# The data's Fourier transform reads the loaded data as two 64-column operands instead of one of 128 from a rearranged copy

## The chip, the cores and the metric

The kernel runs on one core of a Trainium2 chip. The metric is the device time of one execution in microseconds. The five engines are called as in the profile: PE (matrix products; PEld is its loading of the stationary operand), DVE and ACT (the two engines that also read PSUM, where PE writes), POOL, and SP, which here issues nearly all transfers.

## The reference, cut to what matters

The output is a gated mix `g * a + (1 - g) * b` of two branches on the same input x (2048 positions, 512 channels).

```python
g = sigmoid((x * gate_w).sum(-1, keepdims=True))
# branch a: a long convolution along the positions
P = exp(logdA[:, :, None] * l[None, None, :])
K = einsum("dn,dnl,dn->dl", Cc, P, dB).real            # filters, 512 x 2048, from 128 complex states
y = irfft(rfft(u padded to 4096) * rfft(K padded to 4096))[:, :, :L]
a = y + u * Dskip
# branch b: linear attention, 32 heads of 16
q, k, v = x @ wqkv;  pq = q @ w_phi;  pk = k @ w_phi
phi(z) = concat(softmax(z), softmax(-z))
o = (phi(q) @ (phi(k)^T v)) / (phi(q) @ sum phi(k) + 1e-6)
b = o @ wo
```

Both branches are computed in bf16 with f32 sums in PSUM.

## The kernel before

**How the work is listed and ordered.** The class `Plan` holds a list of nodes. Each node names its engine (or two, of which one is chosen), its dependences and the buffers that it takes and drops. `Plan.run` emits the nodes in the order that the long string ORDER gives, two characters a node. The string SIDES chooses, for each node that may run on either of two engines, which one (0 the first, 1 the second). RINGS chooses between two PSUM pools, WARM adds spare matmuls (none here), and FOURS says for each of 16 filter units whether its products are summed by DVE or by PE. So the order on each engine, SP's queue too, is a table written out in advance; each engine works through its own list, and waits where an operand is not there.

**The tables (0 to some 30 us).** `prepare` makes the Fourier tables: W1 for stage A, TB for stage B, TI and TJ for the way back, by sines on ACT from angles made by DVE. `selE` (L456) is a small selection table that may be made by DVE or POOL. The state parameters are turned by PE into PSUM (psri, L367) and DVE multiplies them (the rows p_t, L380). `fold` multiplies the weights of keys and queries by w_phi (wps); its four PSUM results go to WW (keys) and Wqp (queries) by an eviction on ACT or DVE.

**Data's transform (some 40 to 95 us).** The data is loaded by 16 transfers to UD, [128, 64, 128]: partition 32*dj + q, then t, then the channel within a block of 128. `keys_and_spectrum` takes the channels in two halves h. For each half, four copies (L549, `udc`, put on DVE) rearrange UD to `UDp`, [128, 2, 64, 32], so that for each of 32 values of c the pair (e, t) makes one operand of 128 columns with a fixed step of 32 elements. Stage A then runs 8 groups; each group has four matmuls (L560, 128 columns, 256 elements from W1) into one PSUM tile and one eviction to XAu by ACT or DVE. Stage B (L585) multiplies XAu by TB, evicts to xst, and SP writes xst to DRAM as XUd, from where it is read later as XUX. In between, on the same engines, the attention's keys are made: pk (PE), Ek (two exponentials on ACT), Zk (sums on DVE), vr (DVE), kvp (PE).

**The filters and the way back (some 95 to 250 us).** For each of 16 units: ACT makes cs (sines) and E (exponential), DVE makes E's lower half (L1052), two products A (L1099, L1104) and two products R (L1116, L1120). Where FOURS is 0, DVE also adds the products (L1109) and PE has two terms; where it is 1, PE has four terms and the sum is left out. PE multiplies A by R (kps, `kgen_chunk`, L180), the result goes to KD, through stage A (`fft_stage_a`, L187: two matmuls of 64 columns with the same KD operand, at column tiles 0 and 64) to XA, through stage B (L193) to XK. DVE multiplies XK by the loaded XUX (t, L1230 and L1233), PE transforms back (psz), the result Zr goes to DRAM and back as ZT, and psy multiplies it by TJ and adds the attention's result. The last unit, 15, is done alone and without the way through DRAM (Z, L1297 and L1354), split into halves. Queries run beside this: pq, Eq, sums zs, factors apm that go through DRAM to ax, a DVE product of Eq with ax (L909), ops, and the last product with wo (bps).

## Time and profile before

| | us |
|---|---|
| median of 3 runs | 256.0 (255.41 to 258.23) |
| the profiled execution, its own time | 255.41 |
| its span, first to last instruction | 253.6 |
| DVE busy | 225.4 |
| ACT busy | 214.4 |
| PE busy | 195.7 |
| mean granted clock of PE | 0.967 |

The busy times are sums over the span. A group of instructions is shown by line, engine, operation and tile, with its busy time, the mean duration of one, and the idle time of its engine just before with what ended it. Instructions of one engine overlap a little: a DVE row of 1.22 us that follows another starts 1.14 us after it. A stretch of the timeline gives start, length and name, and in brackets the wait before. Where a helper records an operation, many tiles share its line: L146 is every copy on ACT, L148 every copy on DVE, L68 every function on ACT.

### The profile page before, as it was taken

To read this page: it belongs to the slowest core of one execution; us is meant where nothing else is said; L and a number is where in the kernel's file an instruction comes from. 1 tells how busy PE (TensorE), PEld (TensorE's weight loads), DVE (VectorE), ACT (ScalarE), POOL (GpSimd) and SP (SyncE) were. 2 spreads that over 40 slices of the span, in tenths; PEclk is the share of its full clock that TensorE was granted. 3 is DMA by queue.
4 is the path that set the end of the run, shared out by engine and by line. 5 is a ranking of instruction groups with operands and counts; after the bars stand their busy time and mean duration, and the time that the engine had idled before them with its cause. 6 is when DMAs were issued, how large, how long until landed. Compare 5 with 4: busy or idle time off the path is not lost. (4 is left out here: it accounts for less than half of the span.)

```text
span 253.6 us, 9977 instructions
## 1 busy us (share of the span) xinstructions
PE 195.7 (77%) x4459; PEld 133.9 (53%) x4480; DVE 225.4 (89%) x307; ACT 214.4 (85%) x293; POOL 8.8 (3%) x21
## 2 busy tenths in 40 slices
PE   1195599899756558799857876989998989999930
PEld 1043365675534333366536554776686666866620
DVE  6479869799999999999999999999999999997821
ACT  4985699899999999999999999999999999764200
POOL 6042000000000000000000000000000000000000
PEclk9999799999979999999999999999999999999975
DMA  6889896101880259912313365224936589899784
GB/s 159 157 153 207 178 202 136 43 3 39 246 217 3 81 156 267 306 30 77 118 47 121 100 196 216 66 65 119 293 95 219 180 236 248 240 244 183 155 111 83
DMA packets 79658, 38.01 MB, mean 150 GB/s; under 512 B 58624, under 2 KB 74624, under 8 KB 79616
## 3 DMA queue, kind: packets, MB, share of 16 engines
q1 hardware_dynamic: 78272, 37.06, 58.2%
q8 instruction: 34, 0.56, 1.0%
q10 hardware_dynamic: 1344, 0.33, 0.7%
q14 instruction: 8, 0.07, 0.1%
HBM read 21.12 MB, written 13.11 MB: 135 GB/s over the span
## 5 line engine op out<-in xcount | busy, mean ns | idle before, releaser
L68 ACT ACTIVATE cs<-args 128x1024 bf16<-128x1024 f32 x32 | 31.3, 1075 | 0.2 <-PE args L1022 0.2
L180 PE MATMUL kps<-R,A 128*32 128x64 bf16 x1600 | 29.3, 228 | 2.5 <-DVE A L1104 0.9
L180 PEld LDWEIGHTS <-A 128*32 128x32 bf16 x1600 | 27.4, 160 | 6.0 <-issue 1.9
L1099 DVE TENSOR_TENSOR A<-Ctab,Dtab 128x2048 bf16<-128x2048 bf16 x16 | 19.5, 1218 | 0.9 <-PE kps L180 0.9
L1120 DVE TENSOR_TENSOR R<-E,cs 128x2048 bf16<-128x2048 bf16 x16 | 19.5, 1217 | 0.0
L1104 DVE TENSOR_TENSOR A<-Ctab,Dtab 128x2048 bf16<-128x2048 bf16 x16 | 19.5, 1216 | 0.0
L1116 DVE TENSOR_TENSOR R<-E,cs 128x2048 bf16<-128x2048 bf16 x16 | 19.5, 1216 | 0.0
L68 ACT ACTIVATE Ek<-pk 128x512 bf16<-128x512 f32 x32 | 16.5, 609 | 2.8 <-PE pk L695 2.7
L676 PE MATMUL vp<-WW,xT 128*128 128x512 bf16 x47 | 12.7, 423 | 6.7 <-DMA xT<-in_A_u_dram 6.7
L146 ACT CAST XK<-psB 128x1024 bf16<-128x1024 f32 (+1 forms) x16 | 15.9, 1020 | 1.9 <-DVE XK L148 1.8
L68 ACT ACTIVATE Eq<-pq 128x512 bf16<-128x512 f32 (+1 forms) x28 | 16.8, 702 | 0.3 <-PE pq L839 0.2
L68 ACT ACTIVATE E<-args 128x1024 bf16<-128x1024 f32 x16 | 17.0, 1059 | 0.0
L695 PE MATMUL pk<-WW,xT 128*128 128x512 bf16 x57 | 15.1, 406 | 2.3 <-ACT WW L146 1.2
L1230 DVE TENSOR_TENSOR t<-XUX,XK 128x2048 bf16<-128x2048 bf16 x14 | 16.9, 1217 | 0.0
L146 ACT CAST Zr<-psz 128x1024 bf16<-128x1024 f32 x15 | 15.5, 1038 | 1.4 <-PE psz L1262 1.1
L839 PE MATMUL pq<-xT,Wqp 128*128 128x512 bf16 x64 | 15.8, 380 | 0.6 <-ACT Eq L68 0.6
L146 ACT CAST XA<-psA 128x1024 bf16<-128x1024 f32 (+1 forms) x16 | 15.5, 1010 | 0.7 <-DVE XA L148 0.7
L1262 PE MATMUL psz<-t,TI 128*128 128x512 bf16 x52 | 14.9, 380 | 1.3 <-DVE t L1230 0.5
L560 PE MATMUL psA<-W,UDp 128*128 128x256 bf16 x64 | 9.8, 286 | 5.1 <-ACT XAu L146 4.0
L585 PE MATMUL psB<-XAu,TB 64*128 64x128 bf16 x256 | 9.3, 216 | 5.6 <-ACT xst L146 3.3
L65 ACT ACT_TABLE_LOAD x10 | 12.8, 1283 | 0.9 <-PEq L1610 0.7
L146 ACT CAST XAu<-psA 128x1024 bf16<-128x1024 f32 x12 | 12.0, 1023 | 1.3 <-PE psA L560 1.3
(207 smaller groups left out, 467.5 us busy)
## 6 DMA issues: line engine op xcount, KB each, us to landing
XUX<-XUd SPq DMA_DIRECT2D x32, 256.0 KB
XUd<-xst SPq DMA_DIRECT2D x8, 512.0 KB
ax<-apd SPq DMA_DIRECT2D x16, 256.0 KB
Zd<-Zr SPq DMA_DIRECT2D x15, 256.0 KB
ZT<-Zd SPq DMA_DIRECT2D x13, 256.0 KB
UD<-in_A_u_dram SPq DMA_DIRECT2D x16, 128.0 KB
XUd<-xst SPq DMA_DIRECT2D x8, 256.0 KB
out_dram<-xT SPq DMA_DIRECT2D x4, 192.0 KB
```

The source lines that it names most:

```text
L65: return self.nc.scalar.preload_act_table_set(name)
L68: return self.nc.scalar.activation(**kw)
L146: self.nc.scalar.copy(out=o, in_=i)
L180: nc.tensor.matmul(kps[32 * dj:32 * dj + 32, g4, e, :], lhsT=A[:, ka, :, :, d].rearrange("p a b -> p (a b)"), rhs=R[:, kr, d, :], start=(i ...
L695: nc.tensor.matmul(box.ps[:], lhsT=xT[:, st, kt, :], rhs=g.WW[:, kt, :], start=(kt == 0), stop=(kt == 3))
L839: nc.tensor.matmul(box.ps[:, m - m0, :] if late else box.ps[:], lhsT=g.Wqp[:, kt, 128 * m:128 * m + 128], rhs=xT[:, 4 * b:4 * b + 4, kt, : ...
L1099: nc.vector.tensor_tensor(out=c.A[:, 0:2].rearrange("p o a b c -> p (o a) b c"), in0=g.C[U // 8][:, 0:2, :, d0 % 256:d0 % 256 + 32].rearra ...
L1104: nc.vector.tensor_tensor(out=c.A[:, 2:4].rearrange("p o a b c -> p (o a) b c"), in0=g.C[U // 8][:, 1:3, :, d0 % 256:d0 % 256 + 32].rearra ...
L1116: nc.vector.tensor_tensor(out=c.R[:, :, :, 32:64], in0=t.E[:, 1].unsqueeze(1).to_broadcast([128, 2, 32, 32]), in1=t.cs[:], op=ALU.mult)
L1120: nc.vector.tensor_tensor(out=c.R[:, :, :, 0:32], in0=t.E[:, 0].unsqueeze(1).to_broadcast([128, 2, 32, 32]), in1=t.cs[:, ::-1, :, ::-1], o ...
L1230: nc.vector.tensor_tensor(out=box.t, in0=Ls[r0 // ns].X[:], in1=box.XK[:].unsqueeze(1).to_broadcast([128, 2, 1024]), op=ALU.mult)
L1262: nc.tensor.matmul(box.ps[:, hb, :], lhsT=fc.TI[:, k].rearrange("p t h a -> p (t h a)"), rhs=box.t[:, k, 512 * hb:512 * hb + 512], start=( ...
```

## The change

The eight copies to UDp go, and with them the buffer and its slot. Stage A reads UD itself: with e fixed, the 64 values of t are one operand of 64 columns with a step of 128 elements, and each former matmul becomes two, with e = 0 at column tile 0 and e = 1 at column tile 64, into the two halves of the same PSUM partitions. The first of each half waits for the tables' release and the loads of UD instead of the copies. W1, the 256 elements and the evictions stay the same.

The tables ORDER, SIDES and RINGS are made anew for the new list of nodes, and FOURS changes in one place (unit 5: from 0 to 1). In the program that comes of it the order of units, evictions and loads is nearly that of before, and these instructions are on another engine: selE on POOL instead of DVE; one XAu, one KD, one WW and one Zr eviction and one of Ctab on DVE instead of ACT; one Wqp, one XK half, both Z, two halves of xT and two gate scalings (L979, on ACT L977) on ACT instead of DVE; KD of the last unit on ACT in two parts; the sum A of unit 5 is gone and 64 kps matmuls are added. Two output transfers (L1380) are issued by SP instead of ACT. SP issues two of the x transposes ahead of Are, Aim and WW, and the first write of XUd ahead of the loads of statE.

```diff
-    FOURS = ("0111010111011000")
+    FOURS = ("0111110111011000")
...
         X = Bag()
-        en, uc = [], []
-        for k in range(4):
-            def cu(h=h, k=k, X=X):
-                if k == 0:
-                    X.u = g.xau.tile([128, 2, 64, 32], BF16, name="UDp", tag="UDp", bufs=1)
-                o = X.u[:, :, 16 * k:16 * k + 16, :].rearrange("p e t c -> p t e c")
-                P.copy(o, g.UD[:, 16 * k:16 * k + 16, 64 * h:64 * h + 64].rearrange("p t (e c) -> p t e c", e=2))
-            uc.append(P.add(("DVE", "ACT"), "udc", cu, [sx] + uc[-1:], take=(["UDp"] if k == 0 else []), rw=(f"ud{k}", "")))
+        en = []
...
                 for i in range(4):
                     c = 4 * g4 + i
-                    nc.tensor.matmul(box.ps[:, i, :], lhsT=X.u[:, :, :, c].rearrange("p e t -> p (e t)"), rhs=fc.W1[:].rearrange("p i r d -> p (i r d)"),
-                                     start=True, stop=True)
+                    for e in range(2):
+                        nc.tensor.matmul(box.ps[64 * e:64 * e + 64, i, :], lhsT=g.UD[:, :, 64 * h + 32 * e + c], rhs=fc.W1[:].rearrange("p i r d -> p (i r d)"),
+                                         start=True, stop=True, tile_position=(0, 64 * e), skip_group_check=True)
...
-            a = P.add("PE", "psAu", pa, [a] if g4 else uc, take=["ps"] + (["XAu"] if g4 == 0 else []), drop=(["UDp"] if g4 == 7 else []), rw=("W1", ""))
+            a = P.add("PE", "psAu", pa, [a] if g4 else [sx], take=["ps"] + (["XAu"] if g4 == 0 else []), rw=("W1 ud0 ud1 ud2 ud3", ""))
...
-        P = Plan(nc, {"XAu": 1, "UDp": 1, "xst": 3, "Ek": 2, "Zk": 2, "vr": 2, "vb": 2, "acc": 1, "r8": 3, "ax": 1, "nrm": 1, "E": 2, "cs": 4, "A": 1, "R": 2,
+        P = Plan(nc, {"XAu": 1, "xst": 3, "Ek": 2, "Zk": 2, "vr": 2, "vb": 2, "acc": 1, "r8": 3, "ax": 1, "nrm": 1, "E": 2, "cs": 4, "A": 1, "R": 2,
```

## The prediction

> **What bounds the kernel now.** I read the page's busy times first, then ten-microsecond windows, then the waits, then the groups that the change touches, and last the timeline of the tail. The page and its slices:

> ```profile
> PE 195.7 (77%) x4459; PEld 133.9 (53%) x4480; DVE 225.4 (89%) x307; ACT 214.4 (85%) x293; POOL 8.8 (3%) x21
> DVE  6479869799999999999999999999999999997821
> ACT  4985699899999999999999999999999999764200
> PEclk9999799999979999999999999999999999999975
> ```

> Neither vector engine has room from about 45 us on; what they lack of the span lies at the front and in the tail. The windows say it more sharply (columns: stretch, its length, busy us of PE, PE loads, DVE, ACT, POOL, granted clock, DMA share, GB/s):

> ```profile
> 50.00:60.00 10.00, 9.49 (x198) 6.78 (x200) 9.52 (x14) 9.93 (x20) 0.00 (x0) 1.00 0.01 3
> 70.00:80.00 10.00, 5.90 (x35) 3.92 (x37) 9.24 (x17) 9.42 (x11) 0.00 (x0) 0.83 0.48 129
> 130.00:140.00 10.00, 7.21 (x235) 5.78 (x235) 10.00 (x11) 9.97 (x12) 0.00 (x0) 1.00 0.30 107
> 220.00:230.00 10.00, 9.40 (x285) 7.28 (x283) 9.97 (x10) 5.30 (x7) 0.00 (x0) 1.00 0.98 247
> ```

> Over the fifteen windows from 80 to 230 us DVE is busy 148.3 of 150 us. ACT keeps up until 220 and then thins out: DVE feeds the last matmuls, and ACT has slack there. The groups that the change touches, from the groups by shape (busy, mean ns of one, idle before and who ended it):

> ```profile
> L560 PE MATMUL psA<-W,UDp 128*128 128x256 bf16 x64 | 9.8, 286 | 5.1 <-ACT XAu L146 4.0 <-ACT Ctab L146 0.6 <-ACT xst L146 0.5
> L187 PEld LDWEIGHTS <-KD 128*64 128x64 bf16 x256 | 8.0, 109 | 5.2 <-issue 3.7 <-ACT KD L146 0.9 <-DVE KD L148 0.2
> L148 DVE COPY UDp<-UD 128x1024 bf16<-128x1024 bf16 x8 | 2.9, 419 | 0.0
> L456 DVE TENSOR_TENSOR selE<-m,b 128x1024 bf16<-128x1024 bf16 x1 | 1.2, 1224 | 0.0
> ```

> The timeline shows one stage-A group of four columns (0.60 us) and the packed stage A of the filters, 16 matmuls in pairs, followed 0.57 us after its start by the next matmul:

> ```profile
> 46.54 0.60 PE L560 MATMUL psA<-W,UDp 128*128 128x256 bf16 x4 [0.58 <-ACT Ctab L146]
> ...
> 223.93 0.64 PE L187 MATMUL psA<-W,KD 128*64 128x128 bf16 x16
> 224.50 0.39 PE L1262 MATMUL psz<-t,TI 128*128 128x512 bf16 x1
> ```

> **The change part by part.** The profiled execution took 255.41 us (span 253.6, 1.8 around it); the median of the three runs is 256.0, so a sum against 255.4 stands 0.6 below the median. Instruction counts of the changed program come from its order on each engine.

> *Copies.* Eight UDp copies leave DVE. Run together they cost 0.75, 0.75 and 1.43 us by the timeline, 2.93 in all, at 41, 44 and 57 us. SIDES moves one XAu eviction from ACT to DVE: started back to back a 128x1024 eviction costs DVE 1.14 and ACT 0.93. In this stage DVE nets -1.8 and ACT -0.9.

> *Middle of the kernel.* FOURS gives unit 5 four products, so one sum A (L1109) goes, -1.14 on DVE; one KD eviction comes from ACT, +1.14 on DVE and -0.93 on ACT. A 512-wide eviction each way between oT and xT cancels. Up to the last operand of the last filter unit DVE has lost 1.8 and ACT 1.9. Since the two take turns as bound and each loses the same, I take **-1.8**. The ends: 0, if the new order waits as much more, and -4.1, if the whole 2.93 counts, and selE's 1.2 too.

> *Stage A on PE.* 64 matmuls of 128 columns become 128 of 64 columns, in pairs at column tiles 0 and 64, with 256 elements each. Before, one took 107 ns in a run (0.43 for four, the rest of 0.60 is the way through the array). If a pair runs together, it costs the same 107; if in series, 214, which is +0.43 per group and +6.9 over sixteen groups. The nearest row is L187: its eight pairs of 128 elements took 0.57 us, 71 ns a pair, against 107 in series by the same rate. So pairs overlap, with some 18 ns on top; 64 pairs make +1.2 of PE. ACT and DVE waited for this matmul five times (1.3 and 1.4 us in the waits), so 0.07 more per group is up to 0.4 on the path; I take **+0.2**, between 0 and 6.9. The loads read with a step of 256 bytes instead of 64, which no row shows; L180 loads 32 columns with a step of 64 bytes in 17 ns (27.4 us by 1600), so two loads of 64 would be 69 ns, hidden behind 107.
> [...]

> *Unit 5's 64 further kps matmuls*: about 1.2 us by rows of that kind. PE had 2.5 us free in 120:130; I cost them at nothing. Without that cover they add 1.2.

> *Front.* Both WW evictions were on ACT with a Wqp between them; the second ended at 28.93 and the first pk waited for it until 28.99, and ACT's first Ek for pk (1.95). Now DVE takes the second where it did Wqp, 26.90 to 28.11: -0.8. selE goes to POOL: DVE gains nothing, since right after it waits 1.40 for dtc. POOL needs 2.1 to 3.0 us for it (twice its 128x512 rows, 1.05 and 1.50), now beside DVE's f32 products; two DVE rows that ran beside POOL at 17.7 and 19.6 took 1.23 and 1.53 where their like took 0.41 and 0.72, so it may cost 0 to 1.6; I take 0.4, half of one. SP loads two transposes ahead of Are and Aim, and of WW; the same transfers stand ahead of the first vp at 11.43, so nothing. UD issues shift past one pair of pz writes; with the copies gone UD is first needed by psA at 46.5, after issues that ended at 38.5. The first XUd write now precedes statE on SP and holds it until about 62; statE is first read at 99. Front: **-0.4**, from -0.8 to +1.6.

> *Tail.* Two Z, two gate scalings, two halves of xT, one XK and the split KD go from DVE to ACT, one Zr and one Ctab come back: -2.7 on DVE. Little of that is on the path. The second half of unit 15's XK was out at 235.65, but its product t started at 236.48, behind xT (0.41) and a scaling (0.61) that now are ACT's: **-0.8**. Two output transfers move from ACT's queue to SP's, ahead of the last four; SP had 1.3 us free before those at 249.41, the two cost 0.9 to 1.6. PE stands still in mid-group there (2.27 and 1.83 us without a releaser); nothing in the change alters that. Ends -2.7 and +0.3.

> Sum: -1.8 + 0.2 - 0.4 - 0.8 = -2.8, so 255.4 - 2.8 = **252.6**.

> **The rivals.**
> 1. *Pairs in series or loads exposed* (slower). Between 46 and 58 us PE is 95% busy and ACT waits on it; eight groups there, each +0.43, add 3.4 that nothing hides, and in the second half (69 to 82) the groups stand right ahead of their evictions with two buffers, up to another 3.4. Gains of 2.8 are outweighed once a pair costs over 150 ns (64 pairs by 0.044 us); fully in series 252.6 + 6.9 = 259.5. Against it: L187. For it: the step of 256 bytes, which no row shows.
> 2. *The new order gives the time back* (no change). The old order let DVE wait 1.7 us in 150; a new one need only wait 2 to 3 us more, at an em for its ax or at an R for its E, to end at 255.2. More than 5.4 (3.6% of 150) would make it slower by over 1%. For it: ACT sheds little in the middle, and each eviction moved shifts a handover. Against: units, tables and loads follow each other as before.
> 3. *All of DVE's lost work counts* (faster): 225.4 less 6.0 (2.9 + 1.1 + 1.2 plus the evictions' balance), as DVE bounds last: 249.4. Against: ACT is as full until 220.
> That the copies stay is excluded: the program has no UDp.

> **How the numbers follow.** Forecast (251.0 to 254.2 by its terms) 0.52; rival 2 at 254 to 258 0.22, with a third of it near or over +1%; rival 1 0.13; rival 3 0.13. One per cent, what a measurement of this kernel can tell from no change, is 2.6 us: faster means under 252.8. About 0.31 of the forecast's 0.52 lies there, with rival 3 0.44. Slower: rival 1 and a third of rival 2, 0.20. The rest, 0.36, is within 1%. The range 249.4 to 258.4 takes in rival 3, the forecast, rival 2, and the cheaper half of rival 1; the forecast's own is 251.0 to 254.2.

> **What would show it.** Right: no UDp rows; the psA group with 128 matmuls busy 10 to 12 us and a group's four pairs within 0.75 us; DVE busy near 219.5, ACT near 215.3; the first cs about 1 us earlier than 93.4; last kps ending 2 us before 231; DVE still over 98% busy from 80 to 225. Wrong: four pairs taking 1 us and XAu waiting for psA over 5 us in sum (rival 1); DVE waits over 4 us between 80 and 225 (rival 2); Ek no earlier than 30.9 (front); the last t of unit 15 still 6 us after its kps (tail).

## The result and the profile after

The changed kernel takes 258.78 us (median of 20 runs, 256.55 to 261.63) where the kernel before took 255.75 (20 runs, 253.31 to 259.24). The ratio is 1.0137, with a 95% interval of 1.0101 to 1.0173: slower by 1.4%, outside the range of the forecast and on its other side. Ratios here and below leave out executions more than 1.5% above the fastest of their own kernel, so they differ somewhat from the quotient of the medians beside them, and the profiled executions of e9 (257.33 us) and e10 (258.74 us) are among those left out.

The profiled execution took 259.56 us, with a span of 257.8: 4.2 more than before. The page's busy times and slices:

```profile
PE 203.8 (79%) x4608; PEld 139.0 (54%) x4608; DVE 218.6 (85%) x292; ACT 215.9 (84%) x298; POOL 10.3 (4%) x22
DVE  6578378898999997999999999999998899998411
ACT  4988949889999989999999899989987999664310
PEclk9999999999999599999995999799997999999975
```

DVE has lost 6.8 us of work and is 4 points less busy. What it lost in work it spends waiting, and more. Two things differ in the slices: DVE and ACT have eights and sevens in the later ones where there were nines, and PE's clock dips four times instead of twice ahead of the tail. The windows that answer to those shown before, and one more:

```profile
50.00:60.00 10.00, 10.00 (x231) 6.64 (x220) 9.21 (x11) 8.76 (x17) 0.00 (x0) 1.00 0.01 3
70.00:80.00 10.00, 6.15 (x62) 4.29 (x62) 9.90 (x20) 10.00 (x12) 0.00 (x0) 1.00 0.72 196
130.00:140.00 10.00, 6.83 (x209) 5.23 (x198) 10.00 (x10) 9.71 (x12) 0.00 (x0) 0.77 0.35 93
190.00:200.00 10.00, 8.86 (x267) 6.48 (x261) 9.03 (x11) 8.39 (x9) 0.00 (x0) 0.84 0.70 218
220.00:230.00 10.00, 9.97 (x247) 7.86 (x246) 9.93 (x11) 7.48 (x9) 0.00 (x0) 1.00 0.89 202
```

The groups and the timeline of stage A after (UDp has no rows any more):

```profile
L555 PE MATMUL psA<-W,UD 128*64 128x256 bf16 x128 | 11.3, 294 | 4.5 <-ACT XAu L147 2.9 <-DVE XAu L149 0.7 <-ACT xst L147 0.7
...
L457 POOL TENSOR_TENSOR selE<-m,b 128x1024 bf16<-128x1024 bf16 x1 | 1.9, 1898 | 0.1
```

```profile
45.54 0.72 PE L555 MATMUL psA<-W,UD 128*64 128x256 bf16 x8
```

Eight matmuls of 64 columns take 0.72 us where four of 128 took 0.60, so the pairs run together. Stage A is as forecast, and the loss is not in it.

Where is it? Two marks divide the span: the first product A on DVE, which opens the filters, and the last kps on PE, unit 15's. Before and after:

```profile
95.60 1.21 DVE L1099 TENSOR_TENSOR A<-Ctab,Dtab 128x2048 bf16<-128x2048 bf16 x1
...
228.92 1.21 PE L180 MATMUL kps<-R,A 128*32 128x64 bf16 x64
```

```profile
93.85 1.21 DVE L1092 TENSOR_TENSOR A<-Ctab,Dtab 128x2048 bf16<-128x2048 bf16 x1
...
232.30 1.24 PE L181 MATMUL kps<-R,A 128*32 128x64 bf16 x64
```

So the changed kernel is 1.75 us ahead at the first mark, spends 138.5 us between the marks instead of 133.3, and 25.5 from the last kps to the end instead of 24.7. The stage between the marks, called the main stage below, alone lost 5.2 us. The lead does not last: at zj, where DVE next needs the keys, it is 0.9 us (99.83 for 100.72), and at the first product R it is gone (103.91 for 103.84). By then DVE has waited 1.3 us for the keys and made zrow (0.69 us), which stood ahead of the first mark before; on ACT two cs have moved behind the mark (one stands ahead of it, where three did). From the first R to the last kps the loss is 3.3 us (128.4 for 125.1).

DVE's waits between the marks (sum, times, longest), before and then after:

```profile
DVE A L1099 <- PE kps L180: 0.9, 3, 0.5
DVE E L1052 <- ACT E L68: 0.2, 1, 0.2
```

```profile
DVE A L1092 <- PE kps L181: 1.3, 2, 1.0
DVE zj L777 <- PE kvp L758: 1.3, 1, 1.3
DVE t L1223 <- ACT XK L147: 0.9, 1, 0.9
DVE Eq L902 <- DMA ax<-apd: 0.9, 2, 0.6
DVE E L1045 <- ACT E L68: 0.6, 2, 0.4
DVE oT L149 <- PE ops L921: 0.3, 1, 0.3
DVE t L1223 <- DMA XUX<-XUd: 0.3, 1, 0.3
```

They come to 5.6 us where the kernel before had 1.1, and they are spread over seven handovers, from PE, ACT and two kinds of transfer; none is over 1.3 in all. ACT's waits there rose too, from 4.2 to 7.8 us. DVE's work between the marks hardly changed (132.2 us before, 132.9 after, the stage less the waits).

### The profile page after: what moved, and what is told of

Same layout as the page of the kernel before. It is cut to its first block, busy times and chain, and to the rows that moved or that the text cites. A ratio compares the mean times of both kernels' runs of the same rounds, so it can differ in the third digit from the quotient of the medians.

```text
span 257.8 us, 10241 instructions
## 1 busy us (share of the span) xinstructions
PE 203.8 (79%) x4608; PEld 139.0 (54%) x4608; DVE 218.6 (85%) x292; ACT 215.9 (84%) x298; POOL 10.3 (4%) x22
## 5 line engine op out<-in xcount | busy, mean ns | idle before, releaser
L181 PE MATMUL kps<-R,A 128*32 128x64 bf16 x1664 | 30.3, 231 | 2.5 <-ACT XA L147 1.0
L181 PEld LDWEIGHTS <-A 128*32 128x32 bf16 x1664 | 28.6, 160 | 6.0 <-issue 2.5
L1109 DVE TENSOR_TENSOR R<-E,cs 128x2048 bf16<-128x2048 bf16 x16 | 19.5, 1217 | 0.0
L1255 PE MATMUL psz<-t,TI 128*128 128x512 bf16 x60 | 16.3, 396 | 0.9 <-ACT E L68 0.4
L147 ACT CAST Zr<-psz 128x1024 bf16<-128x1024 f32 x14 | 14.2, 1047 | 1.4 <-PE psz L1255 1.4
L555 PE MATMUL psA<-W,UD 128*64 128x256 bf16 x128 | 11.3, 294 | 4.5 <-ACT XAu L147 2.9
L578 PE MATMUL psB<-XAu,TB 64*128 64x128 bf16 x256 | 10.5, 238 | 4.2 <-ACT xst L147 2.7
L578 PEld LDWEIGHTS <-TB 64*128 64x128 bf16 x256 | 8.9, 105 | 7.5 <-issue 6.9
## 6 DMA issues: line engine op xcount, KB each, us to landing
XUX<-XUd SPq DMA_DIRECT2D x32, 256.0 KB
ax<-apd SPq DMA_DIRECT2D x16, 256.0 KB
Zd<-Zr SPq DMA_DIRECT2D x15, 256.0 KB
ZT<-Zd SPq DMA_DIRECT2D x13, 256.0 KB
XUd<-xst SPq DMA_DIRECT2D x8, 256.0 KB
```

What stands on the lines that cost most here:

```text
L147: self.nc.scalar.copy(out=o, in_=i)
L181: nc.tensor.matmul(kps[32 * dj:32 * dj + 32, g4, e, :], lhsT=A[:, ka, :, :, d].rearrange("p a b -> p (a b)"), rhs=R[:, kr, d, :], start=(i ...
L578: nc.tensor.matmul(box.ps[:, c2, sl, :], lhsT=fc.TB[rows, b0:b0 + 2].rearrange("p a b -> p (a b)"), rhs=X.t[rows, k, r0 + sl].rearrange("p ...
L1109: nc.vector.tensor_tensor(out=c.R[:, :, :, 32:64], in0=t.E[:, 1].unsqueeze(1).to_broadcast([128, 2, 32, 32]), in1=t.cs[:], op=ALU.mult)
L1255: nc.tensor.matmul(box.ps[:, hb, :], lhsT=fc.TI[:, k].rearrange("p t h a -> p (t h a)"), rhs=box.t[:, k, 512 * hb:512 * hb + 512], start=( ...
```

## The experiments

The change has three parts that can be taken apart: the operand (two of 64 columns, no copies), the order (with its engines and PSUM rings), and unit 5. An order may be cut at any node: all nodes up to it from one table, the rest from the other. The cuts used are the exchange of the first PSUM pool (`x_psum`, some 30 to 45 us) and the giving back of the loaded data's pool (`x_up`, about 90 us).

The table holds every run; each ratio is against the kernel before on the same chip, whose medians were 256.24 (e1 to e4), 254.78 (e5 to e8), 254.53 (e9 to e12), 254.97 (e13 to e16) and 255.87 (e17, e18). "Main" is the time between the two marks, "waits" DVE's waits in it, "stalls" PE's idle times with the releaser "issue" between 100 and 235 us, all from the one profiled execution.

| run | operand, order | us | ratio (95%) | main | waits | stalls |
|---|---|---|---|---|---|---|
| before | copies, old | 255.75 | 1 | 133.3 | 1.1 | 1.0 |
| after | direct, new | 258.78 | 1.0137 (1.0101 to 1.0173) | 138.5 | 5.6 | 0.8 |
| e1 | direct, old | 256.92 | 1.0123 (1.0047 to 1.0200) | 136.8 | 4.6 | 3.0 |
| e2 | copies, new | 259.09 | 1.0192 (1.0100 to 1.0283) | 137.3 | 3.7 | 2.1 |
| e3 | direct, new to x_up, old | 258.87 | 1.0231 (1.0152 to 1.0309) | 136.7 | 2.5 | 1.7 |
| e4 | direct, old to x_up, new | 256.53 | 1.0112 (1.0025 to 1.0198) | 135.9 | 3.5 | 0.9 |
| e5 | after + 112 instructions | 260.33 | 1.0289 (1.0227 to 1.0350) | 139.8 | 5.5 | 3.1 |
| e6 | e1 + 112 instructions | 256.54 | 1.0077 (0.9997 to 1.0156) | 133.5 | 0.8 | 0.0 |
| e7 | direct, new to x_psum, old | 255.28 | 1.0074 (1.0013 to 1.0134) | 134.2 | 2.2 | 2.2 |
| e8 | direct, new from x_psum to x_up | 255.99 | 1.0099 (1.0046 to 1.0151) | 137.1 | 2.7 | 3.0 |
| e9 | e1 + 128 | 255.91 | 1.0032 (0.9980 to 1.0083) | 133.0 | 0.6 | 0.7 |
| e10 | before + 128 | 257.45 | 1.0023 (0.9972 to 1.0075) | 138.0 | 5.2 | 3.8 |
| e11 | after + 128 | 260.35 | 1.0121 (1.0040 to 1.0202) | 136.5 | 3.9 | 1.7 |
| e12 | e7 + 128 | 254.56 | 1.0018 (0.9977 to 1.0059) | 133.2 | 1.2 | 0.3 |
| e13 | after + 256, 56 of the matmuls large | 259.87 | 1.0162 (1.0099 to 1.0226) | 137.8 | 5.3 | 1.1 |
| e14 | before, copies twice | 256.00 | 1.0031 (0.9990 to 1.0071) | 133.5 | 1.3 | 0.8 |
| e15 | before + 256 | 254.40 | 0.9938 (0.9889 to 0.9988) | 133.7 | 1.5 | 1.5 |
| e16 | after + 256 | 259.03 | 1.0141 (1.0100 to 1.0183) | 136.0 | 3.4 | 0.3 |
| e17 | after + 128, unit 5 old | 258.99 | 1.0236 (1.0152 to 1.0320) | 138.1 | 4.6 | 0.9 |
| e18 | e7, unit 5 new | 255.57 | 1.0072 (1.0029 to 1.0116) | 135.1 | 4.0 | 1.5 |

### Operand and order apart: e1 to e4

The theory drawn from the trace was that the order lost the time in the main stage and the operand cost nothing. e1 puts the order, engines, rings and unit 5 of before under the direct operand:

```diff
-    ORDER = ("2B2E0d0e0g0E0H2H0K002K0I0L2I0j0k0J0h1d2C0i2D07082F012L0a0f0F0G1H19040y0z022J0l030A0B2G0C2M052x0b0M0N11120_100S0T0W0U0Y0X"
+    ORDER = ("000d0g0E190h0H0K2E2F0L2H2K2I2B0F0j0a0I0J2v0M0S0U2J0e110V2C010P0Q0T0W0X0N0O040Y0Z16140y15120_0k02170-10070l2w0R080B0C1a1y"
...
-    FOURS = ("0111110111011000")
+    FOURS = ("0111010111011000")
```

and SIDES and RINGS of before likewise, less the entries of the eight copies. e2 is the kernel before with the tables of after, and the copies entered where their operands are there. e3, e4, e7 and e8 differ from e1 in ORDER, SIDES and RINGS alone (e4 has after's FOURS too).

> The direct two-operand stage A and no copies, but every other instruction in the order, on the engine and in the PSUM ring of the kernel before (unit 5's kernel part as before too). Theory 'order': the operand change itself costs nothing, so 253.5 to 255.8 us (before 255.75), stage A again about 0.72 us for four pairs. Rival 'operand': the doubled matmuls are what costs (through the clock or the queue of TensorE), so 257.5 to 260 us, near the 258.8 of after.

> The order, engines, rings and unit 5 of the kernel after, with the eight copies put back on VectorE (four ahead of each half's stage A) and the 128-column operand. Theory 'order': as slow as after or slower by up to the copies' 3.4 us, 258 to 262 us. Rival 'operand': near the kernel before, 254.5 to 257 us.

> Direct stage A; the new order up to the point where the loaded data's pool is given back (about 90 us), then the old order, engines, rings and unit 5 of the kernel before. If the loss lies in the main stage (the reading of the trace: a lead of 1.75 us at 94 turns into a lag of 3.4 at 230): 252.5 to 255.5 us. If the front's rearranged order carries it: 257 to 260 us.

> Direct stage A; the old order up to the same point, then the new order to the end. If the loss lies in the main stage: 258 to 261 us, with two or more half-rate stretches of TensorE between 94 and 230 and over 4 us of VectorE's waits there. If the front carries it: 253.5 to 256 us.

Both theories missed e1: at 256.92 and 1.0123 the operand in the old order is no gain, and it lies between the two expectations. e2 came in as theory "order" expected: with the copies back, the new order is as slow as after. e3 and e4 came out the other way round from the reading of the trace: it is the new front with the old rest that is slow (258.87), and the old front with the new rest that is nearer to before (256.53, between its two expectations). All four have more waits in the main stage than before. In e1 they have a cause that its PE timeline shows at once:

```profile
191.62 1.97 PE L178 MATMUL kps<-R,A 128*32 128x64 bf16 x110 [1.11 <-issue]
193.53 1.04 PE L1252 MATMUL psz<-t,TI 128*128 128x512 bf16 x3
194.71 0.58 PE L185 MATMUL psA<-W,KD 128*64 128x128 bf16 x13
197.18 0.97 PE L185 MATMUL psA<-W,KD 128*64 128x128 bf16 x19 [1.89 <-issue]
```

Twice PE stops in the middle of a group, with nothing that it waits for. Between the two stops are 110 + 3 + 13 = 126 matmuls, with their loads 252 instructions. The page lists transfers of kind "instruction" on a queue of its own: 34 before and 36 after, each of 16,384 bytes. The programs have 4,480 and 4,608 weight loads with a matmul to each, 8,960 and 9,216 instructions on PE, that is 264 and 256 to a transfer. The stops of e1 end 1.40 and 1.27 us after such a transfer has landed (189.24 to 190.23, 194.17 to 195.90), and so it is with every stop of PE after 100 us in all twenty profiles: each ends 1.2 to 2.0 us after the last of these transfers (1.31 to 1.98 in the seven stops of before and after). So PE stops where its next block of code has not come. The direct operand adds 64 matmuls and 64 loads, half a block, and so moves every later stop to another place in the program.

### Filling PE's idle gaps, and cutting the front: e5 to e8

e5 and e6 were made for the clock: large spare matmuls into unused columns of the bank of kvp, behind each group of stages A and B of the second half.

```diff
+        def spare():
+            nc.tensor.matmul(g.spare, lhsT=ident[:], rhs=fc.TB[:, 1:5].rearrange("p a b -> p (a b)")[:, 0:240], start=False, stop=True, skip_group_check=True)
...
             n.fn()
+            for _ in range(self.SPARE.get(i, 0)):
+                self.spare()
```

> The kernel after with 56 spare matmuls (128x240, into unused columns of a PSUM bank): three behind each stage A group of the second half, four behind each stage B group of it, where TensorE idled 0.6 to 1.7 us between 70 and 91 us. Theory 'clock': the half-rate stretch at 84 to 91 us is the answer to those idle gaps and costs about 2 us by the end; without it 256 to 257.5 us, no half-rate between 80 and 91 us. Rival 'order of the front itself' (waits, not clock): 258 to 260 us even where the clock stays up. Rival 'no effect': the stretch comes all the same.

> The same spare matmuls in the direct kernel with the order of before. Theory 'clock': the half-rate stretch at 71 to 75 us (3.4 us) goes, worth under 1 us: 255 to 257 us (without them 256.9), the mean half-rate time per run lower by 3 us. Rival: they stand in the way of the real groups, 257.5 us and more.

> Direct stage A, the new order only up to the point where the first PSUM pool is exchanged (some 30 to 45 us), then the order of before. If the new front's price of 2 us (new front with old rest 258.9, old front with old rest 256.9) is paid in the preparation: 258.5 to 260 us. If it is paid in stage A, stage B and the keys: 256 to 257.5 us.

> Direct stage A, the order of before up to the exchange of the first PSUM pool, the new order from there to the giving back of the loaded data's pool (about 90 us), then the order of before. The complement of the run before it: 258.5 to 260 us if stage A, stage B and the keys carry the price, with a half-rate stretch of 6.8 us near 80 to 92 us; 256 to 257.5 us if the preparation does.

e5's half-rate stretch at 84 us went, and the kernel became slower (260.33). That did not refute the clock by itself, since the 112 instructions of the spare matmuls had raised the stalls from 0.8 to 3.1 us: the experiment changed two things. e6 was as expected in time (256.54), its stretch at 71 us gone, but its profile had 10.2 us at half rate from 25 us on, ahead of the spare matmuls; its main stage, with 128 + 112 = 240 instructions more than before, had no stall left and 0.8 us of waits. e7 and e8 missed: each half of the new front is no slower than e1 (255.28, 255.99), though both together are (e3, 258.87). That is not settled by these runs: the slowness of e3 has no cause shown.

### The blocks of code: e9 to e12, e15

To test the stalls by themselves, 64 tiny matmuls (8 columns, 128 instructions with the loads) go behind the same groups. In the direct kernel they make the half block whole again; in the kernel before they make the half block without the operand.

```diff
+            nc.tensor.matmul(g.spare[0:32, 0:8], lhsT=ident[:, 0:32], rhs=fc.TB[:, 1, 0:8], start=False, stop=True, skip_group_check=True)
```

> The direct kernel in the order of before, with 64 tiny spare matmuls (8 columns, with their weight loads 128 instructions) behind the groups of stages A and B of the second half, so that from there on TensorE's instruction count is 256 above that of before, one whole block of the fetches. Theory 'fetch': the copies' removal is worth 1 to 2 us, but the 128 instructions that the two operands add move the places where TensorE runs out of fetched instructions (3.0 us of such stalls at 191 to 198 us without the pad, 1.0 in before); with the pad they fall back to where they were: stalls between 100 and 235 us 0 to 1.0 us in all, 253.3 to 255.3 us against 255.3 for before. Rival 'the copies were free': stalls gone or not, 255.5 to 257.5 us.

> The kernel before, copies and all, with the same 64 tiny matmuls: the 128 more instructions alone, half a block. Theory 'fetch': the stalls of the direct kernel in the old order come back (2 to 3 us between 185 and 205), 1 to 2 us slower than before. Rival 'no matter': within 0.7 us of before.

> The kernel after with the same 64 tiny matmuls, half a block. It had only 0.8 us of fetch stalls between 100 and 235 us; theory 'fetch' expects 2 to 3 us with the pad, as the run with 112 more instructions (3.1 us), and 259.5 to 261 us. Rival: the 56 large spare matmuls cost by standing in the way, not by the fetches: 258 to 259.5 us here.

> Direct stage A, the new order up to the exchange of the first PSUM pool, then the order of before, with the pad of one whole block in all. Without the pad 255.3 us, with 2.2 us of fetch stalls. Theory 'fetch': stalls under 1.0 us, 253 to 255 us, the best of all so far. Rival: 255 to 256.5 us.

The stalls follow the count. e10, whose copies, operand and order are those of before, has the stops of e1, in psA two matmuls further on. Its timeline shows what one of them does (PE, then those who wait for it):

```profile
194.24 1.93 PE L181 MATMUL kps<-R,A 128*32 128x64 bf16 x108 [0.87 <-issue]
...
196.10 1.04 PE L1263 MATMUL psz<-t,TI 128*128 128x512 bf16 x3
...
197.29 0.63 PE L188 MATMUL psA<-W,KD 128*64 128x128 bf16 x15
...
200.89 0.66 PE L188 MATMUL psA<-W,KD 128*64 128x128 bf16 x17 [2.97 <-issue]
201.14 1.93 ACT L145 CAST XA<-psA 128x1024 bf16<-128x1024 f32 x2 [2.95 <-PE psA L188]
...
204.93 1.23 DVE L1231 TENSOR_TENSOR t<-XUX,XK 128x2048 bf16<-128x2048 bf16 x1 [2.95 <-ACT XK L145]
```

One stop of 2.97 us is handed on whole: ACT waits 2.95 for psA, and DVE 2.95 for the XK that comes of it. The code transfer ahead of it lands at 199.27. In the kernel before the same 32 psA matmuls ran through in 1.08 us. The same stop in psA lasts 0.47 to 1.89 us in e1, e3, e7 and e8, so 2.97 is the most that it cost in five profiles, in a longer execution than e10's median of 257.45. With the block whole again (e9) DVE's waits in the main stage fall to 0.6, the least of all:

```profile
DVE A L1092 <- PE kps L181: 0.4, 2, 0.2
DVE E L1045 <- ACT E L68: 0.2, 1, 0.2
```

e15 is the control: a whole block of tiny matmuls in the kernel before.

> The kernel before with 128 tiny spare matmuls behind the second half's stages A and B: a whole block of instructions. If the pad itself is free (some 0.2 us of TensorE behind each group, mostly in its waits): within 0.6 us of before, and the stalls of the half block (0.9 and 3.0 us) gone. If it costs: +1 to +2 us, and the direct kernel with a whole block has its gain hidden by it.

The pad is free: 254.40, 0.9938, and the psA group is whole again:

```profile
195.03 1.08 PE L188 MATMUL psA<-W,KD 128*64 128x128 bf16 x32
```

Between half a block and a whole one lie 0.0085 of the ratio in the kernel before (1.0023 and 0.9938), 0.0091 in the direct one (1.0123 and 1.0032) and 0.0056 in the one with the new preparation (1.0074 and 1.0018); the mean, 0.0077, is 2.0 us. From the half-widths of the intervals, put together as roots of squares, each difference is uncertain by 0.007 to 0.009, so only the first stands clear of nothing by itself. By the medians of all executions, each over that of before beside it, the differences are 0.0137, -0.0027 and 0.0019, so the time shows the price less surely than the trace does, in which the main stage is longer with the half block in all three pairs (138.0 for 133.7, 136.8 for 133.0, 134.2 for 133.2). Against their expectations, e9 (255.91) lies in the range of its rival, although its stalls fell as the theory said; e10 is slow as the theory said by its median and like before by its ratio; e12 (254.56) fits both. e11's expectation of 2 to 3 us of stalls missed (1.7). Its median of 260.35 is in the theory's range and 1.6 us above after's, its ratio of 1.0121, which rests on two of its six executions, is not: what the half block costs in the new order is open.

### The copies twice, and the clock by itself: e13, e14, e16

```diff
-                P.copy(o, g.UD[:, 16 * k:16 * k + 16, 64 * h:64 * h + 64].rearrange("p t (e c) -> p t e c", e=2))
+                for _ in range(2):
+                    P.copy(o, g.UD[:, 16 * k:16 * k + 16, 64 * h:64 * h + 64].rearrange("p t (e c) -> p t e c", e=2))
```

> The kernel before with each of the eight copies made twice, 3.3 us more on VectorE between 41 and 62 us. The forecast's middle term (what VectorE does there counts about half) says +1.5 to +2 us on before; if VectorE bound that stage alone, +3.3; rival 'the copies lay beside other work': +0.0 to +0.6.

```profile
L146 DVE COPY UDp<-UD x16: 416/426/429, 42.2 to 61.6; 128x1024 bf16<-128x1024 bf16 x16
```

Eight more copies, some 3.4 us of DVE, cost 1.0031 (0.9990 to 1.0071): 0.8 us, at most 1.8, between the expectations. If taking copies away gives what adding them costs, the eight that the change takes away are worth about a quarter of their time, or a half at the most.

For the clock, e13 has the 56 large spare matmuls and 72 tiny ones, e16 has 128 tiny ones: both add one whole block, and in the window from 80 to 90 us PE is busy 9.28 us in e13 and 8.04 in e16.

```diff
             for _ in range(self.SPARE.get(i, 0)):
                 self.spare()
+            for _ in range(self.TINY.get(i, 0)):
+                self.tiny()
```

> The kernel after with the 56 large spare matmuls of the second half's stages A and B and 72 tiny ones: 256 more instructions, one whole block, so the fetches fall where they did. Theory 'clock costs': no half-rate stretch at 80 to 91 us, fetch stalls between 100 and 235 us under 1.2 us, and 256 to 257.8 us against 258.8 of after. Rival 'clock only goes with it': the stretch gone and 258.3 to 260.5 us.

> The kernel after with 128 tiny spare matmuls at the same places: a whole block, and hardly any activity of the array. Fetch stalls as in after (0.8 us between 100 and 235 us), the half-rate stretch near 84 us still there; 258.3 to 260 us. The run with the large ones against this one gives the price of the half-rate stretch.

The window from 80 to 90 us, e13 first:

```profile
80.00:90.00 10.00, 9.28 (x191) 6.68 (x192) 9.83 (x18) 9.70 (x12) 0.00 (x0) 1.00 0.30 82
```

```profile
80.00:90.00 10.00, 8.04 (x180) 6.43 (x180) 9.83 (x16) 9.47 (x11) 0.00 (x0) 0.69 0.29 80
```

The granted clock is 1.00 against 0.69, and DVE is busy 9.83 us in both. The times are 259.87 and 259.03, and the first A stands at 94.54 and 94.20: the half-rate stretch at 84 us costs nothing that shows, unless the large matmuls themselves cost as much as the clock gave. Ahead of the tail, e13 has 6.8 us at half rate as before had, after had 20.5, and e13 is no faster than after. The rival "clock only goes with it" holds for that stretch as far as this goes. Those in the main stage were not taken away one by one, but it does not go by them: with 3.4 us at half rate between the marks it takes 133.0 to 133.5 us in e6, e9 and e14 (old order) and 139.8 and 136.5 in e5 and e11 (new order).

The clock is not cleared altogether. In the 97 executions of the kernel before that were timed beside e1 to e18, the mean granted clock goes from 0.937 to 0.985, and by a straight line through them 0.01 less goes with 1.2 us more. After's 20 executions had 0.945 on average where those had 0.961, which by that line goes with 2.0 us of the 3 us between the kernels. Whether the lower clock makes the time, or the waits make both, is not shown; against the first, e13's executions had 0.961 too and a median of 259.87.

### Unit 5: e17, e18

e17 against after with 64 tiny matmuls (e18 has the reverse against e7):

```diff
-    FOURS = ("0111110111011000")
+    FOURS = ("0111010111011000")
```

> The kernel after with unit 5's kernel part as in before (64 matmuls fewer, a sum more on VectorE) and 64 tiny spare matmuls behind the second half's stages A and B, so that from unit 5 on the instruction count is that of after. If unit 5 makes the waits: 255.5 to 257 us and VectorE's waits between the first A and the last kps under 2.5 us. If the new order apart from it does: 258 to 260 us and 3.5 us of waits or more.

> Direct stage A, the new order up to the exchange of the first PSUM pool, then the order of before, with unit 5's longer kernel part in the place of a pad: from unit 5 on the count is a whole block above before. If unit 5 is harmless: VectorE's waits between the first A and the last kps 0.6 to 2 us, fetch stalls under 1 us there, 253.3 to 255.3 us. If it makes the waits: 3 us and more of them, 256 to 258 us.

Unit 5 is not what makes the waits of the new order: without its longer part it takes 258.99 and DVE waits 4.6 us. In the old order (e18) the longer part did not bring the time under e12's: 4.0 us of waits, 3.2 of them an A waiting for kps. Those waits are the sign that was named for unit 5 making them, and the time of 255.57 lies between the two ranges. So in the old order unit 5 is not shown to be harmless.

### What stands

Sorted by the table, there are three groups. Old order in the main stage and the code blocks where they were (before, e6, e9, e12, e14, e15): main 133.0 to 133.7 us, waits 0.6 to 1.5. Old order and half a block off (e1, e3, e7, e8, e10): 134.2 to 138.0, waits 2.2 to 5.2. New order in the main stage, whatever the blocks, the operand, unit 5 or the stretch at 84 us (after, e2, e4, e5, e11, e13, e16, e17): 135.9 to 139.8, waits 3.4 to 5.6. Counted from the first R instead of the first A, the three take 124.8 to 125.5, 126.1 to 129.7 and 126.3 to 128.7 us. All eight of the last group wait 0.8 to 1.9 us at zj for kvp and none of the others does, so this is one handover that the new order itself has made worse. The operand by itself, in the old order with the blocks in place, is neither gain nor loss that shows (e9 1.0032, e12 1.0018). Half a block off has its price in the trace in all five, and in the ratio where the pairs above show it. e18 is by itself: the old order with the longer unit 5, 4.0 us of waits. No version beats both kernels by the 1% that can be told; e15 comes nearest with 0.6%, and holds nothing but idle instructions more than before.

## Why the prediction was wrong, point by point

**Middle, -1.8: the step that failed.** Its first part held in the old order. In twelve profiles with the direct operand the first A stands at 94.1 us on average, in four with the copies at 95.4 (left out are e3, e6, e9 and e14 at 96.6 to 98.3; the last three had 10.2 us at half rate from 25 us on; with all four in, it is 94.7 and 96.0). There it also lasts (first R at 101.8 to 102.9 in e1, e7, e12 and e18, 102.8 to 103.8 in before, e10 and e15), while after, 1.75 ahead at the first A, is level with before at the first R. DVE's and ACT's busy times came out as said (218.6 and 215.9 for 219.5 and 215.3). What failed is "Since the two take turns as bound and each loses the same, I take -1.8": work taken from two engines that hand operands to each other shortens the span only if the handovers stay in step. The forecast read which instruction changed engines, and took the order to be "nearly that of before". The new order's handovers made 4.5 us more of waits (5.6 for 1.1), over twice what was to be saved. That is rival 2, and its sign, "DVE waits over 4 us between 80 and 225", is what the trace shows; the forecast gave it 0.22 and named the two places, an em for its ax and an R for its E; the first holds 0.9 of the 5.6 us, and E's lower half, which stands ahead of R, waits 0.6 for ACT's E. It priced more than 5.4 us of waits as slower by over 1%; 4.5 did it, since front and tail gave less than forecast. Which moves of the order make the waits can be read from the traces for zj alone, with 1.3 of the 5.6 us: before, DVE made a product A and the sum between its last vr and zj (98.41 to 100.72), which covered kvp; the new order leaves the sum alone there, and PE puts four pq ahead of the last kvp. For the rest it is open: e4 with the new order from 90 us on waits 3.5 us, at handovers like those of after, and no single part that was undone (copies, unit 5, clock, blocks) brought them under 3.4.

**The copies' worth.** The forecast counted the copies less one eviction, 1.8 us, through to the end. e14 says 0.8 us for 3.4 us of copies, and e9 and e12 with the copies gone are not below before. The end 0 of that term was nearer.

**Stage A on PE, +0.2.** Right in the price: 11.3 us busy (10 to 12 forecast), 0.72 us a group (0.75), 2.0 us of XAu waiting for psA where before had 2.7. Rival 1 is excluded. What the working left out is that 64 more matmuls are 128 more instructions. In the old order those moved the stops for code to places that cost 1.0 to 4.3 us of the main stage in three pairs of profiles; in the changed kernel, where unit 5 adds another 128, the stalls are as before (0.8 and 1.0), so this is not what made it slower.

**Unit 5, nothing.** Right for the changed kernel: e17 without it is no faster (258.99). In the old order e18's 4.0 us of waits leave it open.

**Front, -0.4.** The mechanism was right and its yield given back on the way. Ek began early:

```profile
27.93 1.57 ACT L68 ACTIVATE Ek<-pk 128x512 bf16<-128x512 f32 x3 [0.59 <-PE pk L688]
```

That is 27.93 for 30.89. But the transfers, costed at nothing, were not: the pz writes now stand behind four transposes on SP (three before), and DVE stood for one of them:

```profile
30.48 0.69 DVE L380 TENSOR_TENSOR pt<-pmag,ppy 128x512 bf16<-128x512 f32 x1 [4.06 <-DMA pz<-pt]
```

With that wait, the early keys' gain of 3 us is down by 45 us to 1.4 (DVE's vr at 44.23 for 45.62), by when 1.5 us of copies had gone from DVE and ACT's pb (1.07 us) was still to come where it had been made before; psA starts 1.0 earlier (45.54 for 46.54). selE on POOL took 1.90 (2.1 to 3.0 estimated).

**Tail, -0.8.** Wrong, and the tail as a whole came out at +0.8: from the last kps to the second t of unit 15 it takes 7.7 us after and 7.6 before. The scalings did leave DVE, but PE's own order put another group ahead of psA:

```profile
233.49 1.04 PE L935 MATMUL bps<-wo,oT 128*128 128x512 bf16 x4
...
234.58 1.03 PE L935 MATMUL bps<-wo,oT 128*128 128x512 bf16 x4
...
235.75 0.64 PE L188 MATMUL psA<-W,KD 128*64 128x128 bf16 x16
```

Both parts of KD are out at 234.29 and psA starts 1.46 later; before, it started 0.24 after KD, with the second bps group behind it. Then ACT makes both halves of XK one after the other (1.07 us) where DVE and ACT had one each. Moving work off DVE was counted; the order on PE, and who else could have done it, were not.

**Rival 3** is out: DVE lost 6.8 us of work in all, and the kernel became slower.

## What to carry to other kernels

When a change comes with an order made anew, price the order as a change of its own: walk each handover between the engines, the queue's too, since a tuned order with 1.1 us of waits in 133 has more to lose than a few copies can give. Put the old order under the new operand, and the new order under the old operand, before blaming either. And before blaming an edit on PE, move its instruction count by half a block and by a whole one: a stop for code that falls on the path cost as much here, in one profile, as the edit was forecast to gain (2.97 us in e10, for 2.8). A mark in the timeline tells of a lead only if the same work stands ahead of it in both orders.

## What the runs showed of the hardware that was not expected

PE's half-rate stretches ahead of the tail (granted clock 0.50) are, in before and after, 3.4 us long or twice that (6.8 at 84 us in after), and differ from profile to profile: 20.5 us in after, 6.8 in before. The profile of after, with 13.7 us more of them, is 4.2 us longer in all, and e13, with 6.8 us at half rate ahead of the tail, is no faster than after (259.87 for 258.78). By the line through the 97 executions of before, 1 us more at half rate goes with an estimated 0.24 us: it takes 0.002 off the mean clock of a span of 254 us, and 0.01 goes with 1.2 us.
